# 128 tokens of expert 0 computed during the gating of the last batch

## The chip, the cores and the metric

One core of one Trainium2 chip. The time is the device time of one execution in microseconds; the span is the time from the first to the last instruction of the profiled execution. Inputs are drawn once, so the number of tokens of each expert is fixed.

## What is computed

Causal attention with a decay bias over 4 batches of 8 heads and 576 tokens, then a mixture of 8 experts with one expert for each token, then a dense feed-forward layer with a squared ReLU. The weights of the last layer come as float64.

```python
# attention: scores + min(-(cum_i - cum_j), 0), causal, softmax, times v
x = attn_out.transpose(0, 2, 1, 3).reshape(2304, 512)
logits = x @ w_gate
e_idx = argmax(logits, axis=1)                 # one of 8 experts
gate_w = softmax(logits)[e_idx]; eom = sigmoid(x @ w_output_gate)
for e in range(8):
    h = maximum(x[e_idx == e] @ w1[e], 0)      # 512 -> 1024
    out[e_idx == e] = gate_w * eom * (h @ w2[e])   # 1024 -> 512
g = maximum(out @ w_in, 0) ** 2                # 512 -> 2048
result = g @ w_out                             # 2048 -> 512
```

With these inputs expert 0 gets 334 tokens: 252 from the first three batches and 82 from the last.

## The kernel before

**Order.** The order of the instructions is written out by hand: `at(key, fn)` puts a step on a list, the list is sorted by key, and each engine runs its instructions in that order. Steps on other engines are kept apart by semaphores. In the attention part a key counts work units of head pairs (16 pairs, 7 units each). In the expert part a key counts h blocks: expert g has the steps 8g to 8g + 7.

**Attention and gating.** As soon as a batch of attention is done, `emit_gate` finds for each token its expert and its rank among the tokens of that expert (`s_lg` to `s_rk`), marks ranks in one-hot tiles (`s_r1`, L789) and turns them into a table of token numbers by small matmuls (`s_tb`, L799). The table has three chunks of 128 ranks for each expert. For batches 0 to 2 all this lies beside the attention of the next batch. For the last batch nothing lies beside it: `s_tbl` adds the earlier batches' table, and `gather(0, [c])` fetches the rows of expert 0 for chunk c from DRAM by an indirect DMA on POOL (L289). In the waits TensorE runs dummy products of 512 columns (`warm` L348, `warm_h` L1462).

**Ranking of the experts.** Expert 0 is always first. The other seven are sorted by their number of tokens (`perm_steps`), since each place in the order has a fixed capacity: `CAPS`, 352, 320, 304, 304, 288, 288, 272 and 256 columns. The result is the tile `slot_v`: which expert has which place and where its output starts. SyncE reads it into registers (`load_regs`, L182), seven for the experts and later seven for the places, ahead of the weight loads that use them. `p_tbl` sorts the table itself (`tbl_p`) for the gathers of the later experts.

**Experts.** `x_trans` transposes the gathered rows (L1116) and splits them into a high and a low float32r half on ScalarE (L1122) and the vector engine (L1127). `emit_h` (L1211) makes 128 of the 1024 hidden units by 12 matmuls: 3 products of halves times 4 pieces of 128 inputs. The weights are the stationary operand, the tokens are the moving columns. `emit_hv` (L1221, L1222) applies the ReLU and splits again, and `emit_y` (L1253), two steps behind, adds 12 matmuls into four accumulators. These are called blocks of 12 below. `y_store` puts the result transposed into `yT_d`, sorted by place.

**Weights.** Those of expert g + 1 are loaded during expert g, eight jobs of 512 KB on SyncE's queue (L232), through three staging buffers and one spare. Each job is split into halves by ScalarE (L241) and the vector engine (L245). Beside them 16 pieces of the float64 weights of the last layer are converted (`cv_load` to `cv_store`, every 3.55 steps from step 1.2). The gather of expert 1 (`gather(1)`) uses the only tile for gathered rows.

**PSUM.** In attention the eight banks belong to three rings (`s`, `s2`, `t`). In the expert part they are `z0` to `z7`: four accumulators and a ring of four.

Of the kernel before, what the change touches and what calls it, by code (L numbers as in the profile page):

```python
# [24 lines left out]
P = 128  # L25
# [46 lines left out]
    cvb=0.4,  # L72
    cvm=0.7,
    cvp=3.55,
    cv0=1.2,
# [12 lines left out]
def attention_moe_ffn_kernel(  # L88
# [72 lines left out]
    gap = const.tile([P, 1], F32, name="gap")  # L161
    slot_v = const.tile([1, 3, E], I32, name="slot_v")
# [117 lines left out]

    def gather(g, cs=None):
        if cs is None or cs[0] == 0:
            xr_t[g] = xr_p.tile([P, CH, DM], F32, tag="xr", name="xr")
        t = xr_t[g]
        for c, n in enumerate(rows_of(g)):
            if cs is not None and c not in cs:
                continue
            idx = tbl_i[0:n, c * E:c * E + 1] if g == 0 else tbl_p[0:n, c, g:g + 1]
            nc.gpsimd.indirect_dma_start(  # L289
                out=t[0:n, c, :], out_offset=None, in_=x_d[:, :],  # L290
                in_offset=bass.IndirectOffsetOnAxis(ap=idx, axis=0))
# [10 lines left out]

    with tc.manual_schedule():
        with ExitStack() as actx:
# [7 lines left out]
            ps_s = actx.enter_context(tc.tile_pool(name="ps_s", bufs=K_["S"], space=PSUM))  # L312
            ps_t = actx.enter_context(tc.tile_pool(name="ps_t", bufs=6 - K_["S"] - K_["O"], space=PSUM))
            ps_o = actx.enter_context(tc.tile_pool(name="ps_o", bufs=K_["O"], space=PSUM)) if K_["O"] else ps_t
# [411 lines left out]
            def emit_gate(b, tg, gk):  # L726
# [36 lines left out]
                def s_pr():  # L763
                    pr = ps_o.tile([P, 512], F32, tag=o_tag, name=o_tag)
# [4 lines left out]
                    for t in range(NB - 1):  # L769
                        nc.tensor.matmul(  # L770
                            prv[:, t + 1:NB], lhsT=onesb, rhs=oh[:, t:t + 1].to_broadcast([P, NB - 1 - t, E]),
                            start=False, stop=(t == NB - 2))

# [12 lines left out]
                def s_r1(t, c0=0, c1=CH):  # L786
                    if t == 0 and c0 == 0:
# [4 lines left out]
                def s_tb(c0=0, c1=CH):  # L792
                    tb = T["tb", c0] = bank("o")
# [64 lines left out]
                steps = [s_lg, s_mx, s_eq, s_cand, s_ix, s_oh, s_pr, s_oid, s_tm, s_rk]  # L858
                if last:
# [7 lines left out]
                else:  # L867
                    steps += [partial(s_r1, t) for t in range(NB)] + [s_tb, s_tbl]
                rest = [s_cs, s_ca, s_dl, s_zs, s_pe, s_se, s_rr, s_gq]
                if last:  # L870
                    late_steps.extend(rest[2:])
                    steps += rest[0:2]
                else:
                    steps += rest
                for i, st_ in enumerate(steps):
                    at(tg + (0.001 * i if last else gk[i]), st_)
                if last:
                    at(tg + 0.0055, warm, K_["wm"][3])
                    at(tg + 0.0145, warm, K_["wm"][4])
# [193 lines left out]
            for i, job in enumerate((k, i, h) for k, i in half_jobs(0, "a") + half_jobs(0, "b") for h in range(2)):  # L1073
# [3 lines left out]
                at(tw + 0.5, part_lo, *job)  # L1077
            emit_tasks()

        stg_p = ctx.enter_context(tc.tile_pool(name="stg", bufs=3))  # L1080
# [6 lines left out]
        ps_z = ctx.enter_context(tc.tile_pool(name="ps_z", bufs=1, space=PSUM))  # L1087
        ring = [4, 4, 0]

        def bank_z(i):  # L1090
            return ps_z.tile([P, 512], F32, tag=f"z{i}", name=f"z{i}")

        def bank_x():
            ring[2] += 1
            return bank_z(ring[0] + ring[2] % ring[1])

# [11 lines left out]
        xp_t = {}  # L1108

        def x_pe(g, c, k0=0, k1=KD):  # L1110
            if c == 0:
                xt_t[g] = xt_p.tile([P, 2, KD, TT], F32R, tag="xt", name="xt")
            r = rows_of(g)[c]
            ps = bank_x()
            for kk in range(k0, k1):
                nc.tensor.transpose(  # L1116
                    ps[:, (kk - k0) * r:(kk - k0 + 1) * r], xr_t[g][0:r, c, kk * P:(kk + 1) * P], ident[0:r, 0:r])
            xp_t[g, c, k0] = ps[:, 0:(k1 - k0) * r].rearrange("p (k n) -> p k n", k=k1 - k0)

        def x_hi(g, c, k0=0, k1=KD):  # L1120
            r = rows_of(g)[c]
            nc.scalar.copy(out=xt_t[g][:, 0, k0:k1, c * P:c * P + r], in_=xp_t[g, c, k0])  # L1122

        def x_lo(g, c, k0=0, k1=KD):
            r = rows_of(g)[c]
            xt = xt_t[g]
            nc.vector.tensor_tensor(  # L1127
                out=xt[:, 1, k0:k1, c * P:c * P + r], in0=xp_t.pop((g, c, k0)),
                in1=xt[:, 0, k0:k1, c * P:c * P + r].bitcast(F32), op=ALU.subtract)
# [73 lines left out]
        def emit_h(g, e, f, fl):  # L1203
            n = sum(rows_of(g))
# [12 lines left out]
        def emit_hv(g, f):  # L1217
            n = sum(rows_of(g))
# [21 lines left out]
        def emit_y(g, e, f, fl, nf, f0=0):  # L1240
# [5 lines left out]
            if g < E:  # L1246
                n = CAPS[g]
# [47 lines left out]
        def emit_yv(g):  # L1295
            ysb = ysb_t[g] = y_p.tile([P, 4, TT], F32, tag="ysb", name="ysb", bufs=1)
            if g < E:
                n = CAPS[g]
# [13 lines left out]
        def y_store(g):  # L1312
            ysb = ysb_t.pop(g)
            if g < E:
                n = CAPS[g]
                dst = yT_d.rearrange("(k p) n -> p k n", p=P)
                nc.sync.dma_start(
                    out=dst[:, :, 0:n] if g == 0 else dst[:, :, ds(reg_o[g], n)], in_=ysb[:, :, 0:n])
# [9 lines left out]

        scr = {}

        def gt2(nm, shape, rows=P):
            if not scr:
                scr["t"] = y_p.tile([P, 4, TT], F32, tag="ysb", name="ysb", bufs=1).rearrange("p a n -> p (a n)")
                scr["n"] = 0
            n0 = scr["n"]
            scr["n"] = n1 = n0 + int(np.prod(shape))
# [350 lines left out]
```

## Time and profile before

| | |
|---|---|
| median of 3 runs | 877.02 us (875.78 to 878.04) |
| profiled execution | 876.1 us |
| its span | 874.3 us |
| TensorE matmul busy | 846.9 us, 97% |
| vector engine busy | 521.5 us, 60% |
| ScalarE busy | 449.7 us, 51% |
| GpSimd (POOL) busy | 254.5 us, 29% |
| DMA moved | 113.13 MB |
| mean granted TensorE clock | 0.991 |

Times in the rows below are microseconds from the start of the span unless they are marked ns. PE is TensorE, PEld its weight loads, DVE the vector engine, ACT ScalarE, SP SyncE. A busy time is that of an engine as a whole; a matmul's record overlaps the next one, so the cost of a stream of matmuls is read from starts, or from the chain of work. L12 is line 12 of the kernel.

### The profile page before, as it was taken

Reading aid. Unit: us, or ns where it says so; the run is one execution under the profiler, and the core shown is the slowest. Engines: PE = TensorE matmul, PEld = TensorE weight load, DVE = VectorE, ACT = ScalarE, POOL = GpSimd, SP = SyncE. Lnnn points to the kernel's source line nnn. Section 1 sums busy time; section 2 is a strip of 40 time slices with the busy share of each in tenths; the row PEclk is TensorE's granted clock in tenths of the full one; section 3 lists DMA queues with packets and bytes.
Section 4 is the critical chain, followed back from the end, with each engine's and each line's share of the span. In section 5 each row is a group of like instructions: output and inputs, shape, how many; then the busy total and the mean of one; then the engine's idle time right before and its main releaser. Section 6 shows DMA issues by size and latency. Waiting matters only on the chain.

```text
span 874.3 us, 15070 instructions
## 1 busy us (share of the span) xinstructions
PE 846.9 (97%) x5381; PEld 750.2 (86%) x5381; DVE 521.5 (60%) x1182; ACT 449.7 (51%) x1001; POOL 254.5 (29%) x302
## 2 busy tenths in 40 slices
PE   7999999999899999999999999999999999999993
PEld 5877777776589999999999999999999999999993
DVE  8667777978666687777866667664333333232221
ACT  6687878987254566565655546443333232222221
POOL 4322344543125655556302232331101001001001
PEclk9999999999999999999999999999999999999997
DMA  6666677652178798988983433321010110000001
GB/s 157 142 161 140 150 178 177 171 135 79 47 243 273 237 265 235 281 267 254 293 231 118 145 108 109 97 85 61 25 49 36 47 63 37 1 1 37 0 1 39
DMA packets 112500, 113.13 MB, mean 129 GB/s; under 512 B 66017, under 2 KB 83425, under 8 KB 112418
## 3 DMA queue, kind: packets, MB, share of 16 engines
q1 hardware_dynamic: 106162, 97.23, 40.4%
q0 software_dynamic: 3664, 9.62, 3.2%
q10 hardware_dynamic: 2592, 5.24, 1.7%
q8 instruction: 44, 0.72, 0.4%
q14 instruction: 38, 0.31, 0.1%
HBM read 80.50 MB, written 23.32 MB: 119 GB/s over the span
## 4 chain that ended last, share of the span: by engine, by line
PE 55%; issue 30%; ACT 5%; DVE 4%; POOL 3%; DMA 1%; SPq 1%; POOLq 0%; DVEq 0%; ACTq 0%
PE z L1211 19%; PE z L1253 12%; PE z L1262 7%; PE t L580 5%; PE s L483 4%; PE t L543 4%; ACT p L527 2%; POOL out_dram L1321 2%; ACT sta L423 1%; PE z L1116 1%; PE t L396 1%; ACT pt L562 1%; PE s L618 1%; PE t L675 1%; DMA stg<-in_moe_w_dram 1%
## 5 line engine op out<-in xcount | busy, mean ns | idle before, releaser
L1211 PE MATMUL z<-xt,w 128*128 128x384 f32 (+6 forms) x1920 | 334.2, 323 | 0.4 <-DVE h L1222 0.4
L1211 PEld LDWEIGHTS z<-xt,w 128*128 128x128 f32 x1920 | 312.3, 188 | 9.3 <-DVE h L1222 0.6
L1262 PE MATMUL z<-w,h 128*128 128x512 f32 x864 | 214.9, 393 | 0.0
L1262 PEld LDWEIGHTS z<-w,h 128*128 128x128 f32 x864 | 160.7, 188 | 29.3
L1231 DVE SCALAR_TENSOR_TENSOR r<-z,r 128x384 f32<-128x384 f32 x96 | 53.3, 556 | 128.4 <-ACT r L1230 127.5
L1230 ACT ACTIVATE r<-z 128x384 f32<-128x384 f32 x96 | 47.1, 491 | 149.9 <-PE z L1211 147.6
L1253 PE MATMUL z<-h,w 128*128 128x304 f32 (+5 forms) x768 | 115.0, 299 | 0.0
L1253 PEld LDWEIGHTS z<-h,w 128*128 128x128 f32 x768 | 108.0, 188 | 0.0
L1179 POOL TENSOR_TENSOR cvm<-cvm,cva 128x512 f32<-128x512 f32 x32 | 43.6, 1363 | 195.3 <-DVE cva L1175 153.8
L1238 DVE TENSOR_TENSOR h<-r,h 128x384 fp32r<-128x384 f32 x96 | 60.9, 635 | 50.3 <-ACT h L1237 47.4
L1321 POOL DMA_INDIRECT out_dram<-ysb,tok_m x18 | 17.4, 968 | 245.5 <-ACT ysb L1308 183.2
L527 ACT ACTIVATE p<-p,nm 128x128 f32<-128x128 f32 (+3 forms) x144 | 84.2, 589 | 4.8 <-DVE nm L510 4.7
L1237 ACT CAST h<-r 128x384 fp32r<-128x384 f32 x96 | 49.3, 513 | 63.3 <-DVE r L1231 63.0
L510 DVE CUSTOM_DVE_ANT_0 p<-s,mask 128x128 f32<-128x128 f32 (+3 forms) x128 | 59.6, 486 | 28.8 <-PE s L483 27.7
L543 PE MATMUL t<-ident,p 128*128 128x128 f32 x400 | 69.4, 283 | 3.1 <-DVE sta L427 1.1
L245 DVE TENSOR_TENSOR w<-stg,w 128x1024 fp32r<-128x1024 f32 x49 | 68.7, 1401 | 0.8 <-ACT w L241 0.8
L543 PEld LDWEIGHTS t<-ident,p 128*128 128x128 f32 x400 | 44.5, 141 | 19.7 <-ACT p L527 7.3
L241 ACT CAST w<-stg 128x1024 fp32r<-128x1024 f32 x49 | 51.3, 1046 | 8.7 <-DMA stg<-in_moe_w_dram 6.0
L1222 DVE SCALAR_TENSOR_TENSOR h<-z,h 128x304 fp32r<-128x304 f32 (+5 forms) x64 | 29.6, 462 | 42.0 <-ACT h L1221 41.3
L444 POOL CAST stb<-sta 64x1152 fp32r<-64x1152 f32 x28 | 31.4, 1149 | 79.5 <-PE s L483 47.4
L1180 POOL TENSOR_TENSOR cvm<-cvs,cvm 128x512 f32<-128x512 f32 x32 | 53.3, 1666 | 2.5
L483 PE MATMUL s<-sta 128*64 128x288 f32 (+4 forms) x204 | 49.8, 341 | 3.4 <-ACT sta L423 1.3
(219 smaller groups left out, 1025.7 us busy)
## 6 DMA issues: line engine op xcount, KB each, us to landing
stg<-in_moe_w_dram SPq DMA_DIRECT2D x42, 512.0 KB
cv<-in_moe_w_out_dram SPq DMA_DIRECT2D x16, 512.0 KB
stx<-in_moe_w_dram SPq DMA_DIRECT2D x14, 512.0 KB
cv<-in_moe_w_in_dram SPq DMA_DIRECT2D x14, 512.0 KB
xr<-yT_d SPq DMA_DIRECT2D x8, 768.0 KB
qk<-in_q_dram SPq DMA_DIRECT2D x32, 128.0 KB
qk<-in_k_dram SPq DMA_DIRECT2D x32, 128.0 KB
v<-in_v_dram SPq DMA_DIRECT2D x32, 128.0 KB
```

The lines of the kernel that those rows point to most:

```text
L241: nc.scalar.copy(out=w_parts(job)[0], in_=raw[job])
L245: nc.vector.tensor_tensor(out=lo, in0=raw.pop(job), in1=hi.bitcast(F32), op=ALU.subtract)
L483: nc.tensor.matmul(ps[0:mw, d0:d0 + nn], lhsT=ql[r, m0:m0 + mw], rhs=kl[r, c0:c0 + nn], start=(i == 0 and (tail or n == 0)), stop=(done an ...
L510: nc.vector.tensor_tensor_reduce(out=dst, in0=src, in1=msk, scale=-1.0, scalar=3.0e38, op0=ALU.add, op1=ALU.min, accum_out=nm[:, c:c + 1])
L527: nc.scalar.activation(out=pt[:, cs], in_=pt[:, cs], func=AF.Exp, scale=-1.0, bias=nm[:, c:c + 1], accum_out=rs[:, r:r + 1])
L543: nc.tensor.transpose(tp[:, i * P:(i + 1) * P], pt[:, j0:j0 + P], ident)
L1180: nc.gpsimd.tensor_tensor(out=m, in0=sq, in1=m, op=ALU.add)
L1211: nc.tensor.matmul(ps[:, 0:n], lhsT=wa[:, zw, kk, fl * P:(fl + 1) * P], rhs=xt[:, zx, kk, 0:n], start=(i == 0), stop=(i == 3 * KD - 1))
L1231: nc.vector.scalar_tensor_tensor(out=gg, in0=ps[:, 0:TT], scalar=0.0, in1=gg, op0=ALU.max, op1=ALU.mult)
L1238: nc.vector.tensor_tensor(out=ht[:, 1], in0=gg, in1=ht[:, 0].bitcast(F32), op=ALU.subtract)
L1253: nc.tensor.matmul(y_acc[g][d][:, 0:n], lhsT=wb[:, zw, fl, d * P:(d + 1) * P], rhs=ht[:, zh, 0:n], start=(f == 0 and i == 0), stop=(f == n ...
L1262: nc.tensor.matmul(acc, lhsT=ht[:, zh, c * P:(c + 1) * P], rhs=wb[:, zw, fl, :], start=(first and i == 0), stop=(last and i == 2))
```

## The change

The first three batches already fix the 128 first ranks of expert 0. Their row numbers are copied to `idx0` after the gating of batch 2 and gathered in the last head pair (from the part of `x_d` that the first three batches wrote). In the gating of the last batch these 128 tokens go through both layers of expert 0, with the tokens as the stationary operand and 512 weight columns moving: `early_h` (two halves of 12 matmuls), `early_hr`, `early_ht`, `early_hs` (ReLU, transposes, split), `early_y` (24 matmuls into one bank), `early_copy` and `early_store`. Tiles of finished head pairs hold the operands. The eight `z` banks are opened ahead of this gating instead of behind attention. The dummy products `wm[3]` to `wm[8]` go.

Expert 0 itself then has 224 columns (`cols_of`) instead of 352, from chunks 1 and 2. The order within the gating is new: ranks, table and gather of chunk 1, then chunk 2, then the counts and the ranking of the experts (`p_cnt`, `p_first`), then chunk 0 of the table, which only later experts need, and `p_tbl`. The rest of the ranking's small operations (`m_ov`, `m_off`, `m_cnt`, `m_end`) are spread over the steps 2.95 to 5.95, and `pos_tokens` goes from step 1.5 to 6.95. One more condition (`seen0`) sends the kernel to its general loop if the first three batches have fewer than 128 tokens of expert 0. The registers are read one per expert, each ahead of the loads of that expert. The conversion of the last layer's weights starts at step 4.0 with 3.45 steps between pieces, and the transposes of expert 1's rows come 1.2 steps later.

```diff
-    cvp=3.55,
-    cv0=1.2,
+    cvp=3.45,
+    cv0=4.0,
...
+    def cols_of(g):
+        return sum(rows_of(g)) - P * first_of(g)
...
-            idx = tbl_i[0:n, c * E:c * E + 1] if g == 0 else tbl_p[0:n, c, g:g + 1]
+            if g == 0:
+                idx = tbl_i[0:n, c * E:c * E + 1] if c else idx0
+            else:
+                idx = tbl_p[0:n, c, g:g + 1]
...
                 if last:
-                    ahead = 2
-                    for c in range(CH):
-                        steps += [partial(s_r1, t, c, c + 1) for t in range(ahead if c else 0, NB)]
-                        steps.append(partial(s_tb, c, c + 1))
-                        if c + 1 < CH:
-                            steps += [partial(s_r1, t, c + 1, c + 2) for t in range(ahead)]
-                        steps += [partial(s_tbl, c, c + 1), partial(gather, 0, [c])]
...
+                    eh, ey = partial(early_h, 0), partial(early_h, 1)
+                    steps += [partial(eh, 0, 9), *pr, s_n3, partial(eh, 9, 12), partial(early_hr, 0), partial(ey, 0, 5)]
+                    steps += [*r1[1], tb[1], partial(early_ht, 0), *r1[2][0:2], tl[1], partial(gather, 0, [1])]
+                    steps += [partial(early_hs, 0, 0), partial(ey, 5, 8), *r1[2][2:], tb[2], partial(ey, 8, 12)]
+                    steps += [partial(early_hr, 1), s_cs, s_ca, p_cnt, tl[2], partial(gather, 0, [2]), s_dl]
+                    steps += [partial(early_hs, 0, 1), partial(early_y, 0, 2), partial(early_ht, 1)]
+                    steps += [partial(early_hs, 1, 0), partial(x_pe, 0, 1), start_scr, *p_first, partial(early_y, 2, 4)]
+                    steps += [partial(early_hs, 1, 1), *r1[0], partial(x_pe, 0, 2)]
+                    steps += [partial(early_y, 4, 8, ((0, 0), (0, 1))), tb[0], partial(early_y, 4, 8, ((1, 0),))]
+                    late_steps.extend([tl[0], p_tbl, *rest[3:]])
...
+                if b == B - 2:
+                    at(tg + gk[16] + 0.05, nc.vector.tensor_copy, idx0, tbl[:, 0:1])
+                    at(tg + gk[16] + 0.06, gather, 0, [0])
...
-                    at(tg + 0.0055, warm, K_["wm"][3])
-                    at(tg + 0.0145, warm, K_["wm"][4])
...
+            def early_h(half, i0, i1):
+                if i0 == 0:
+                    EA["h", half] = bank_z(3 + half)
+                wa = half_views((0, "a"))
+                seq = [(zw, zx, kk) for zw, zx in ((0, 0), (1, 0), (0, 1)) for kk in range(KD)]
+                for i in range(i0, i1):
+                    zw, zx, kk = seq[i]
+                    nc.tensor.matmul(
+                        EA["h", half], lhsT=x0[:, zx, kk], rhs=wa[:, zw, kk, 512 * half:512 * half + 512],
+                        start=(i == 0), stop=(i == 3 * KD - 1))
...
+            te = len(K_["order"]) * (NPAIR - 1)
+            at(te + K_["ext"], early_xt)
+            at(te + K_["exs"], early_xs)
...
+            emit_tasks(NU * (NPAIR - 1) + K_["lpv"][0][-1] + K_["xe"] + 0.01 - 1e-6)
+            pctx.close()
+            zp.append(ctx.enter_context(tc.tile_pool(name="ps_z", bufs=1, space=PSUM)))
...
-        at(-0.74, load_regs, range(1, E), 0, reg_e, E - 1)
-        for i, fn in enumerate(late_steps + then):
+        at(-1.1, load_regs, [1], 0, reg_e, E - 1)
+        for i, fn in enumerate(late_steps[0:2]):
+            at(-0.7 + 0.01 * i, fn)
+        for i, fn in enumerate(late_steps[2:]):
             at(-0.5 + 0.01 * i, fn)
...
-        at(0.3, gather, 1)
+        for i, fn in enumerate(p_late):
+            at(2.95 + i, fn)
+        for c in (1, 2):
+            at(-1.0 + 0.1 * c, x_hi, 0, c)
+            at(-0.99 + 0.1 * c, x_lo, 0, c)
+        at(-0.65, early_copy)
+        at(0.5, early_store)
+        at(-0.6, gather, 1)
...
+            if g:
+                at(n0 + NF + 1.0, load_regs, [g], 1, reg_o, NT)
+            if g > 1:
+                at(n0 - NF - 1.5, load_regs, [g], 0, reg_e, E - 1)
...
-                w_job(job, max(ta - K_["wld"], -0.7), ta + K_['wh'], ta + K_['wl'])
-        at(1.5, pos_tokens)
+                w_job(job, -0.7 if g == 0 and i < 4 else ta - K_["wld"], ta + K_['wh'], ta + K_['wl'])
+        at(6.95, pos_tokens)
```

## Rows read from the trace of the kernel before

**Rows 1.** The page, busy tenths in 40 slices of the span:
```profile
PE   7999999999899999999999999999999999999993
...
DMA  6666677652178798988983433321010110000001
```
**Rows 2.** TensorE in order of time: start us, us, engine, line, operation:
```profile
220.53 1.90 PE L580 MATMUL t<-pt,v 128*64 128x320 f32 x20
...
223.82 2.32 PE L348 MATMUL t<-onesb 128*128 128x512 bf16 x10
225.98 0.18 PE L766 MATMUL t<-carryb,onesb 128*128 128x40 bf16 x1
...
227.68 0.63 PE L799 MATMUL t<-oid_all,r 128*128 128x8 bf16 x14
...
230.45 2.32 PE L1462 MATMUL z<-onesb 128*128 128x512 bf16 x5 [0.26 <-DVE tbl_i L808]
...
237.76 6.15 PE L1211 MATMUL z<-xt,w 128*128 128x352 f32 x36
```
**Rows 3.** Busy time by stretch: length, PE, PEld, DVE, ACT, POOL, granted clock, DMA:
```profile
224.00:228.00 4.00, 4.00 (x35) 2.07 (x33) 3.35 (x19) 1.89 (x10) 0.32 (x1) 1.00 0.27 78
228.00:230.00 2.00, 1.56 (x23) 0.98 (x20) 1.85 (x11) 0.00 (x0) 1.22 (x1) 1.00 0.00 0
230.00:234.00 4.00, 3.74 (x15) 2.00 (x16) 0.62 (x4) 0.22 (x1) 2.35 (x4) 0.57 0.60 176
...
252.00:272.00 20.00, 19.88 (x125) 19.59 (x126) 16.70 (x23) 11.42 (x18) 8.05 (x6) 1.00 0.76 254
```
**Rows 4.** Chain of work: start us, us, what (352, 272, 256, 512 columns):
```profile
262.62 1.93 PE z L1253 x12
...
340.17 0.44 PE z L1116 x4
...
424.07 1.50 PE z L1211 x12
...
447.59 1.44 PE z L1211 x12
...
465.35 2.08 PE z L1262 x9
```
**Rows 5.** TensorE in expert 0 and at expert 1's first block, in order of time:
```profile
246.07 0.63 PE L1116 MATMUL z<-ident,xr 128*128 128x128 f32 x4 [0.23 <-DMA xr<-x_d,tbl_p]
...
251.08 0.66 PE L1116 MATMUL z<-ident,xr 128*128 128x128 f32 x4 [0.54 <-DMA xr<-x_d,tbl_p]
252.12 2.19 PE L1211 MATMUL z<-xt,w 128*128 128x352 f32 x12 [0.39 <-DVE h L1222]
...
268.25 1.93 PE L1211 MATMUL z<-xt,w 128*128 128x320 f32 x12
```
**Rows 6.** The vector engine in order of time:
```profile
219.25 0.69 DVE L564 COPY pt<-t 128x512 f32<-128x512 f32 x1
220.64 0.42 DVE L564 COPY pt<-t 128x256 f32<-128x256 f32 x1 [0.69 <-PE t L543]
...
239.19 0.16 DVE L1390 CAST slot_v<-ysb 1x8 int32<-1x8 f32 x1
...
251.98 1.22 DVE L245 TENSOR_TENSOR w<-stg,w 128x1024 fp32r<-128x1024 f32 x1
...
262.63 1.93 DVE L245 TENSOR_TENSOR w<-stx,w 128x1024 fp32r<-128x1024 f32 x1
```
**Rows 7.** ScalarE in order of time, end of attention and gating:
```profile
221.34 0.48 ACT L562 COPY pt<-t 128x384 f32<-128x384 f32 x1 [2.06 <-PE t L580]
...
223.74 2.15 ACT L661 ACTIVATE xs<-s,rca 128x64 f32<-128x64 f32 x10 [0.89 <-DVE lw L637]
```
**Rows 8.** POOL, then SyncE's queue, in order of time:
```profile
228.71 1.22 POOL L289 DMA_INDIRECT xr<-x_d,tbl_i  x1 [2.32 <-DVE r L789]
...
244.48 5.00 SPq L232 DMA_DIRECT2D stg<-in_moe_w_dram  x3
```

More of the change, by code (lines that the diff above doesn't have):

```diff
@@ L72 @@
     cvb=0.4,
+    ext=4.4,
+    exs=5.6,
     cvm=0.7,
-    cvp=3.55,
-    cv0=1.2,
+    cvp=3.45,
+    cv0=4.0,
     cvl=2.5,
@@ new lines, in attention_moe_ffn_kernel, with p_cnt, gt2 @@
+    R = {}
+    def p_cnt():
+        cps = bank_x()
+        nc.tensor.matmul(cps[:, 0:E], lhsT=onesb, rhs=carryb, start=True, stop=True)
+        R["cps"] = cps[:, 0:E]
+    scr = {}
+    keep = {"pv": "eq", "sv": "cand", "pm": "lg"}
+    def gt2(nm, shape, rows=P):
+        if nm in keep:
+            v = g_p.tile([P, 80 if keep[nm] == "lg" else 40], F32, tag=keep[nm], name=keep[nm])
+            n0, n1 = 0, int(np.prod(shape))
+            return split(v[0:rows, n0:n1], shape)
+        if "t" not in scr:
+            scr["t"] = y_p.tile([P, 4, TT], F32, tag="ysb", name="ysb", bufs=1).rearrange("p a n -> p (a n)")
+            scr["n"] = 0
+        n0 = scr["n"]
+        scr["n"] = n1 = n0 + int(np.prod(shape))
+        return split(scr["t"][0:rows, n0:n1], shape)
@@ L772, in s_pr, with s_n3 @@
                             start=False, stop=(t == NB - 2))
+                def s_n3():
+                    nc.scalar.copy(out=seen0, in_=T["pr"][0:1, 0, 0:1])
                 def s_oid():
@@ L786, in s_r1 @@
                 def s_r1(t, c0=0, c1=CH):
-                    if t == 0 and c0 == 0:
+                    if "r1" not in T:
                         T["r1"] = r1_p.tile([P, NB, CH * P], BF16, tag="r1", name="r1")
@@ new lines, in early_hr, with early_ht, early_hs @@
+            def early_hr(half):
+                EA["r", half] = qk_p.tile([P, 2 * QM + 2 * D], F32, tag="qk", name="qk")[:, 0:512]
+                nc.scalar.activation(out=EA["r", half], in_=EA["h", half], func=AF.Relu)
+            def early_ht(half):
+                ps = EA["t", half] = bank_z(half)
+                for i in range(4):
+                    nc.tensor.transpose(ps[:, i * P:(i + 1) * P], EA["r", half][:, i * P:(i + 1) * P], ident)
+            def early_hs(half, z):
+                ps = EA["t", half].rearrange("p (k n) -> p k n", k=4)
+                f = slice(4 * half, 4 * half + 4)
+                if z == 0:
+                    nc.scalar.copy(out=hT0[:, 0, f], in_=ps)
+                else:
+                    nc.vector.tensor_tensor(
+                        out=hT0[:, 1, f], in0=ps, in1=hT0[:, 0, f].bitcast(F32), op=ALU.subtract)
@@ new lines, in early_y @@
+            def early_y(f0, f1, zs=((0, 0), (0, 1), (1, 0))):
+                if "y" not in xp_t:
+                    xp_t["y"] = bank_z(2)
+                wb = half_views((0, "b"))
+                for zh, zw in zs:
+                    for f in range(f0, f1):
+                        nc.tensor.matmul(
+                            xp_t["y"], lhsT=hT0[:, zh, f], rhs=wb[:, zw, f, :],
+                            start=(f == 0 and zh == zw == 0), stop=(f == FE // P - 1 and zh == 1))
+            te = len(K_["order"]) * (NPAIR - 1)
```

293 lines of the change are left out of this document (155 added, 138 removed).

## Prediction

> **What bounds the kernel now.** I read the slices of the page first. TensorE is busy in nine tenths or more of nearly every slice, and the DMA engines are at seven to nine tenths from slice 12 to 21, where the experts run [rows 1]. So the time is TensorE's own work plus the few places where that work isn't useful. Next I read TensorE in order of time around the gating of the last batch [rows 2]. The last product of attention ends at 222.4 us (220.53 + 1.90), the transposes behind it end at 224.0, and the first block of expert 0 starts at 237.76. In these 13.8 us TensorE runs 29 dummy products of 512 columns (L348 and L1462), the small products of the ranking, and 12 transposes. The chain here goes through the vector engine and a gather, not through TensorE. Busy time by stretch shows the same [rows 3]: from 228 to 230 us TensorE is busy 1.56 of 2.00 us with small table products, and from 230 to 234 us its granted clock is 0.57, near the lower of its two levels (1.2 GHz); before and after it is 1.00, the upper one (2.4 GHz).
>
> From 237.76 us the chain is one block of 12 matmuls after another with almost no gap. A block costs 1.93 us at 352 columns, 1.50 at 272 and 1.44 at 256; nine products of 512 columns cost 2.08; four 128 x 128 transposes cost 0.44 [rows 4]. Expert 0 is 16 such blocks: eight h and six y blocks lie before expert 1's first block at 268.25, two y blocks behind it. Its cost is 268.25 - 237.76 + 2 x 1.93 = 34.35 us [rows 2, 4, 5].
>
> **The change, part by part.** The 128 earliest tokens of expert 0 come from the first three batches, so their rows are known before the last batch is gated. Their two layers move into the 13.8 us.
>
> *Removed.* The 29 dummy products. They held nothing up for more than about 2.3 us [rows 2], but they fill the gap, and real work takes their place.
>
> *Added to the gap.* 24 products of 512 columns for h and 24 for y: 48 x 0.231 = 11.1 us (0.231 is 2.08/9 [rows 4]). Eight transposes of h and eight of the two late chunks of x at 0.11: 1.75. The ranking and table products stay: 30 at 0.63/14 = 0.045 are 1.35 [rows 2], and the counts add some 0.2. Sum 14.4 us. Against this stands the other chain. The table of chunk 1 is first now; in before its counterpart went to the gather at 228.71, and transposed rows were at hand some 4 us later [rows 8]. In the new order, writing the engines' queues out with durations from the rows, chunk 1 is gathered at about 229 and wanted at 233.5, chunk 2 is gathered at 230.5 and wanted at 235. TensorE becomes the bound of this stretch and doesn't wait: the new end is its start plus 14.4.
>
> *The start moves too.* The early x must be transposed and split in the last head pair: one transposed group in a gap of TensorE, one copy on ScalarE, one 0.69 us subtraction on the vector engine. The latter is queued ahead of the two copies at 219.25 and 220.64 [rows 6]. The first copy then ends about 1.35 us later, the second about 0.65 (it had 0.69 us of idle ahead of it). The product at 220.53 runs over that second copy; after its own first 0.7 us it needs it, so I charge 0.5 us, between nothing and 0.7. The ScalarE copy lies in that engine's idle 2.06 us [rows 7] and costs nothing. Start 224.5, expert 0 at 238.9: **1.1 us later** than now.
>
> *Expert 0 shrinks* from 352 to 224 columns. No row has 224. From 352 to 272 a column costs (160.8 - 125.0)/80 = 0.45 ns per matmul, from 272 to 256 only (125.0 - 120.0)/16 = 0.31, and a transpose with 128 columns against a full 128 x 128 weight tile still costs 110 [rows 4]. So the curve flattens: a straight line gives 106 ns, the cost of 256 columns gives 120. I take 114, since the last slope is already lower than the line's. 192 x 0.114 = 21.9 us. Add 12 transposes of expert 1 (1.3), four of the early result on its way out (0.44), and 1.0 of stalls; the stalls now are 0.23, 0.54 and 0.39 [rows 5], from the gather of expert 1 and from ScalarE waiting for weights. Sum 24.6 against 34.35: **9.7 us less**.
>
> The Trainium skill, "TensorE: Matmul & The Clock Gate", section "LDWEIGHTS (loading the stationary operand)", gives a weight load a time that depends only on its columns, 128/1.2 = 107 ns. By it an estimate of 192 x 0.107 = 20.5 us would be the least that expert 0 can cost, and a further cut of columns would bring nothing; the bend between 272 and 256 agrees with it, while no row here shows the floor itself.
>
> *Registers, ranking, weights.* The ranking of the experts now runs on the vector engine before the last table, so the slots are known near 233.7 instead of 239.3 [rows 6]. One register is read instead of seven ahead of the first weights, which were issued at 244.48 [rows 8]; now about 234.5, except that the third staging buffer lies on memory which the early h occupies until 238.9, and SyncE's queue holds the fourth behind it. Expert 1's weights thus have more lead than before, and expert 0 being 10 us shorter doesn't starve it. The other registers are read one per expert on SyncE, each in front of that expert's loads; a read there is under a microsecond and the queue is ahead of need. The gather of expert 1 is held until the early result has left its tile (about 240.8), yet was issued at 242.45 before; its transposes are 1.2 steps later as well.
>
> *Vector engine.* Twenty small operations (0.16 each, as the cast at 239.19 [rows 6], 3.2 us) move from the quiet start of expert 0 into its steps 3 to 7. From 252 to 272 us the vector engine is busy 16.70 of 20.00 [rows 3], weight splits taking 1.22 to 1.93 each [rows 6]. The same work, 0.8 less for narrower h, plus 3.2, is 19.1 us in a stretch that TensorE now does in 15. The overhang is 4 us. An h block's low half is wanted some 4.7 blocks after it, 6.4 us, so I cost the overhang at nothing beyond the 1.0 of stalls.
>
> **Sum.** 9.7 - 1.1 = 8.6 us less. The profiled execution took 876.1 us (span 874.3), so 867.5; the median of the runs is 0.9 above it, so **868.4 us**.
>
> **Rivals.**
> *The weight-load floor:* 224 columns cost what 256 do, 0.120. For it: the bend. Against: the transposes' 0.110. 192 x 0.006 = 1.1 more: 869.5. The skill page above is the rule behind it.
> *The vector engine becomes the bound in expert 0:* the 4 us of overhang come through in place of the 1.0 charged: 871.4. For it: 16.70 of 20.00. Against: the 6.4 us of slack.
> *Banks not free:* the early products want accumulators that ScalarE's ten scaled copies (223.74 + 2.15) still read [rows 7]. The stream starts 1.9 us later: 870.3. Against: those copies read another ring than the first early h.
> *The clock:* on the other side. If TensorE is granted the lower level over the early stream, as it was from 230 to 234 us [rows 3], 14.4 us of work double: 868.4 + 14.4 = 882.8, slower. It decides once more than 8.6 us, 60% of the stream, run at that level; half the stream gives 875.6, no change. Against: the fall followed small table products, and the stream is now dense.
>
> **How the numbers follow.** Forecast 0.57, floor 0.12, vector engine 0.17, banks 0.06, clock over half 0.04, over all 0.04. Low end: pitch 106 (-1.5), early products at a dummy's (225.98 - 223.82)/10 = 0.216 [rows 2] (-0.7), no late start (-0.5), no stalls (-1.0): 864.7, so 864.5. High end: the floor (+1.1) with the vector overhang (+3.0) and a little: 873.0. This leaves out the clock cases and some of the tails. A measurement of this kernel can tell about 0.3% (2.6 us) from no change: faster 0.92, same 0.04, slower 0.04.
>
> **What would show it.** TensorE without an idle stretch from 224 to 239 us at granted clock 1.00; expert 0's blocks at 1.37 us; expert 1's first h block near 260; everything behind it the same length, shifted by about 8.6 us. It is wrong if blocks stay at 1.44 or more, if expert 0's blocks wait on the vector engine or on DMA, if TensorE waits for the gathered chunks, or if a later expert, whose weights share DMA engines already at nine tenths, gives some of it back.

## The result: slower, and the profile after

The changed kernel takes 888.02 us (median of 4 runs, 881.3 to 890.66), the kernel before in the same comparison 877.06 (875.78 to 878.04). The ratio is 1.0113, 95% interval 1.0085 to 1.0141: 1.1% slower, where 1.0% faster was forecast. The profiled execution took 888.55 us (span 886.9).

I cut both spans at the same seven events and subtracted. The last column is the kernel of the eighth experiment ("all mends"), put here so that the stages need be listed only once.

| stage, us | before | after | after - before | all mends |
|---|---|---|---|---|
| up to the last head pair's first product (x20) | 209.64 | 210.75 | +1.11 | 212.02 |
| to the end of attention's last transposes | 14.34 | 15.32 | +0.98 | 14.74 |
| gate: to expert 0's first block | 13.78 | 17.74 | +3.96 | 14.06 |
| expert 0, to expert 1's first block | 30.49 | 26.29 | -4.20 | 22.06 |
| expert 1 | 29.94 | 32.28 | +2.34 | 28.79 |
| experts 2 and 3 | 56.05 | 56.05 | 0.00 | 56.06 |
| experts 4 and 5 | 53.57 | 61.44 | +7.87 | 53.59 |
| experts 6 and 7 | 49.70 | 49.81 | +0.11 | 49.82 |
| dense layers | 416.8 | 417.2 | +0.4 | 417.3 |
| span | 874.3 | 886.9 | +12.6 | 868.4 |

The first row isn't the change's: this stage took between 209.4 and 212.0 us in the traces of all kernels here, and longest in that of the fastest.

The slices of the page of after, to be read against [rows 1]:

```profile
PE   7999999999889999998999999999999999999993
...
DMA  6676677652178887988894442331020120000001
```

TensorE now has eights in the slices of 222 to 266 us (gate, expert 0) and of 399 to 421 us (expert 5). Before it had one eight here, in the slice of 219 to 240 us, and nines behind it.

TensorE of after in order of time: start us, us, engine, line, operation, and in brackets the idle time ahead of it and what ended it. These answer to [rows 2, 5].

```profile
222.25 0.44 PE L691 MATMUL t<-ident,p 128*128 128x128 f32 x2 [0.69 <-DVE pt L712]
222.62 1.90 PE L728 MATMUL t<-pt,v 128*64 128x320 f32 x20
...
228.04 3.34 PE L1064 MATMUL z<-w,sta 128*128 128x512 f32 x9 [1.97 <-ACT xs L809]
...
243.81 1.50 PE L1419 MATMUL z<-xt,w 128*128 128x224 f32 x12
...
254.32 0.63 PE L332 MATMUL z<-ident,xr 128*128 128x128 f32 x4 [1.88 <-DMA xr<-x_d,tbl_p]
...
267.32 1.60 PE L1419 MATMUL z<-xt,w 128*128 128x224 f32 x12 [1.40 <-DVE xt L1335]
...
290.18 3.29 PE L1419 MATMUL z<-xt,w 128*128 128x320 f32 x12 [1.91 <-DVE h L1430]
...
377.76 2.02 PE L1419 MATMUL z<-xt,w 128*128 128x288 f32 x12 [1.96 <-DVE h L1430]
...
405.08 2.02 PE L1419 MATMUL z<-xt,w 128*128 128x288 f32 x12 [2.51 <-DVE h L1430]
```

Four things are to be seen. The new subtraction stands ahead of a copy and costs TensorE 0.69 us at 222.25. The early stream doesn't begin behind attention's transposes at 226.07 but 1.97 us later, released by the last of ScalarE's scaled copies, `xs`. Expert 0 has two stops of over a microsecond (1.88 and 1.40) and three of 0.35 to 0.50, 4.6 us in all. And TensorE stops for 1.9 to 2.5 us once in expert 1 and twice in experts 4 and 5, where little of the change lies but the new timing of the conversion of the last layer's weights.

Busy time by stretch in the gate of after: length, PE, PEld, DVE, ACT, POOL, granted clock, DMA share, GB/s (compare [rows 3]):

```profile
226.00:228.00 2.00, 0.07 (x1) 0.00 (x0) 1.69 (x10) 1.99 (x10) 0.00 (x0) 1.00 0.14 42
228.00:230.00 2.00, 1.96 (x7) 1.59 (x8) 0.08 (x1) 0.00 (x0) 0.32 (x1) 0.77 0.41 109
230.00:232.00 2.00, 2.00 (x12) 1.28 (x10) 0.31 (x2) 0.11 (x1) 0.00 (x0) 0.50 0.03 4
232.00:234.00 2.00, 2.00 (x14) 1.47 (x13) 1.31 (x8) 0.64 (x2) 0.00 (x0) 0.88 0.00 0
```

Behind the idle stretch TensorE's granted clock goes to 0.50, the lower of its two levels, while it is busy all the time. The first nine early products take 3.34 us; where the clock stays at 1.00 the same record shows 2.31 (third experiment).

The clock falls again behind each of the three later stops. The stretches of the lowest clock there:

```profile
292.00:294.00 2.00, 2.00 (x9) 2.00 (x8) 2.00 (x4) 0.53 (x3) 1.81 (x3) 0.52 0.36 51
...
380.00:382.00 2.00, 2.00 (x11) 2.00 (x10) 2.00 (x4) 1.76 (x3) 1.84 (x2) 0.50 0.78 230
...
408.00:410.00 2.00, 2.00 (x10) 1.72 (x9) 2.00 (x4) 0.00 (x0) 1.89 (x2) 0.50 0.81 281
```

With the neighbouring stretches (granted clocks 0.63 and 0.52; 0.82, 0.50 and 0.83; 0.64 and 0.50), what TensorE loses is 2.0 us times the sum of what is missing from 1.00: 1.7 us each time. So the 7.87 us of experts 4 and 5 are stops of 1.96 and 2.51 us and 3.4 us of low clock. In expert 1 it is a stop of 1.91 and 1.7 of low clock.

The chain of waits of after, from expert 0 on: start us, us, what. Between the lines the chain is TensorE's blocks and short steps of ScalarE, the vector engine and POOL.

```profile
246.40 9.87 DMA yT_d<-h
...
256.35 0.36 ACT h L1429
...
279.01 9.09 DMA w_in_d<-cvm
...
368.71 7.04 DMA w_out_d<-cvm
...
395.41 8.14 DMA w_out_d<-cvm
```

Before, the chain here was one block after another. Now it runs through four DMA stores of 256 KB. The first is the early result on its way out: it holds one of the three `h` tiles until 256.27, and ScalarE, whose next ReLU wants that tile, stands for 7.40 us:

```profile
256.35 0.36 ACT L1429 ACTIVATE h<-z 128x224 fp32r<-128x224 f32 x1 [7.40 <-PE z L1419]
```

The record names the product that feeds the ReLU, but that had been done since 248.4 us; the chain gives the store, and the fourth experiment bears it out. The other three are converted pieces of the last layer's weights. There is one `cvm` tile; ScalarE's multiplication for the next piece must wait until the store of the last has read it, and ScalarE's queue keeps its order, so the ReLUs behind it wait too, then the vector engine, then TensorE.

What SyncE's queue of after waited for between 232 and 262 us (us in total, times, longest us), then the queue itself in order of time, to be read against 244.48 of [rows 8]:

```profile
SPq L186 <- DVE slot_v L402: 11.1, 1, 11.1
SPq L236 <- PE z L1092: 3.1, 1, 3.1
```
```profile
244.12 1.46 SPq L236 DMA_DIRECT2D stg<-in_moe_w_dram  x3
```

All of expert 1's first weights are issued at 244.12, when the last early product (L1092) is done, not near 234.5. So 2 MB of weights, the gather, the early store and the first pieces to be converted move together: from 244 to 254 us the DMA share is 0.90.

### The profile page after: what moved, and what is told of

It is laid out like the page before. It is cut to its first block, busy times and chain, and to the rows that moved or that the text cites. A ratio compares the mean times of both kernels' runs of the same rounds, so it can differ in the third digit from the quotient of the medians.

```text
span 886.9 us, 15158 instructions
## 1 busy us (share of the span) xinstructions
PE 848.3 (96%) x5412; PEld 752.7 (85%) x5412; DVE 525.1 (59%) x1186; ACT 452.4 (51%) x1008; POOL 260.8 (29%) x302
## 4 chain that ended last, share of the span: by engine, by line
PE 51%; issue 29%; ACT 6%; DVE 5%; DMA 4%; POOL 3%; POOLq 0%; ACTq 0%; DVEq 0%; SPq 0%
PE z L1419 17%; PE z L1461 9%; PE z L1470 7%; PE t L728 5%; PE s L631 4%; PE t L691 4%; ACT p L675 2%; POOL out_dram L1529 2%; DMA w_out_d<-cvm 2%; DMA yT_d<-h 1%; ACT sta L571 1%; DMA w_in_d<-cvm 1%; PE t L544 1%; PE z L1064 1%; ACT pt L710 1%
## 5 line engine op out<-in xcount | busy, mean ns | idle before, releaser
L249 DVE TENSOR_TENSOR w<-stg,w 128x1024 fp32r<-128x1024 f32 x49 | 71.7, 1466 | 3.9 <-ACT w L245 3.9
L1388 POOL TENSOR_TENSOR cvm<-cvs,cvm 128x512 f32<-128x512 f32 x32 | 55.8, 1744 | 2.5
```

The costliest lines, as they stand in the source:

```text
L249: nc.vector.tensor_tensor(out=lo, in0=raw.pop(job), in1=hi.bitcast(F32), op=ALU.subtract)
L1388: nc.gpsimd.tensor_tensor(out=m, in0=sq, in1=m, op=ALU.add)
```

## The experiments

**Theory:** five separate costs were missed. (a) Opening the new PSUM banks waits for every reader of the old ones. (b) The stop makes the clock fall. (c) The staging buffers wait in the same way for the early operands, so that expert 1's loads collide with everything else of expert 0. (d) The early result's store holds an `h` tile. (e) Converting pieces from step 4.0 every 3.45 steps makes ScalarE wait for stores. **Rivals:** the conversion alone; the vector engine in expert 0; or the early computation itself costs more than it saves, in which case no mend of its surroundings makes it faster than before. Each kernel is an edit of the changed one unless it says otherwise. Line numbers are those of the changed kernel.

### The conversion as it was

```diff
-    cvp=3.45,
-    cv0=4.0,
+    cvp=3.55,
+    cv0=1.2,
```

> The changed kernel with the old timing of the float64 conversion (first piece at step 1.2, one every 3.55 steps). Theory C: in the changed kernel ScalarE waits in its order for the store of the piece before (25.1 us of idle ahead of L1375, against 13.6 us in the kernel before), since 3.45 steps leave 1.15 instead of 1.25 steps between a store and the next use of its only tile; the ReLU behind it is late, TensorE stops, and 7.9 us are lost in experts 4 and 5. Then the old timing gives 879 to 882 us and no stop of TensorE in experts 4 and 5. Rival D: the shorter expert 0 loads the DMA engines more and any timing stalls; then it stays at 886 to 890 us.

876.66 us (874.54 to 882.69), ratio 1.0010 (0.9992 to 1.0028), faster than the theory expected. Experts 4 and 5 take 53.59 us and expert 1 28.79. So all of the 7.87 us, and more than the 2.34, hang on these two numbers. Expert 0 is no shorter than in after (26.42 against 26.29). It stops for another reason now; ScalarE and TensorE of this kernel in order of time:

```profile
250.66 0.68 ACT L1371 ACTIVATE cvs<-cv 128x512 f32<-128x512 f32 x1 [5.97 <-DMA cv<-in_moe_w_in_dram]
```
```profile
251.63 1.15 PE L1461 MATMUL z<-h,w 128*128 128x224 f32 x8 [3.05 <-ACT h L1429]
```

The earlier conversion waits for its own load, which moves in the same crowd as the weights.

### The change's conversion in the kernel before

```diff
-    cvp=3.55,
-    cv0=1.2,
+    cvp=3.45,
+    cv0=4.0,
```

> The kernel before with nothing changed but the timing of the conversion (first piece at step 4.0, one every 3.45 steps). Theory C: the stops in the later experts appear here too, without any early tokens: 882 to 887 us. Rival D: 877 us, no difference.

877.91 us (876.41 to 882.59), ratio 1.0023 (1.0008 to 1.0039), between the rival's 877 and the theory's 882 and nearer to the rival. TensorE of this kernel:

```profile
396.04 1.85 PE L1211 MATMUL z<-xt,w 128*128 128x288 f32 x12 [2.34 <-DVE h L1222]
```

One stop of 2.34 us, and experts 4 and 5 take 56.33: the interval costs the kernel before 2.8 us there, and 1.1 come back in expert 0 (29.35 in place of 30.49). So the conversion does harm by itself, but a third of what it does in the changed kernel. The traces show what the third is: one stop in place of two, and the granted clock stays at 1.00 behind it. Why the changed kernel gets more stops from the same interval isn't shown.

### Banks that wait tile by tile

```diff
-            zp.append(ctx.enter_context(tc.tile_pool(name="ps_z", bufs=1, space=PSUM)))
+            zp.append(ctx.enter_context(tc.tile_pool(name="ps_z", bufs=1, space=PSUM, reuse_waits="tile")))
```

> The changed kernel with the eight z banks waiting bank by bank for their last use in attention, not for the last use of any bank of the pools they replace. Theory P: the 1.97 us wait of the first early product for ScalarE's scaled copies is such a wait of the whole pool, the bank itself was free; then the early stream starts 2.0 us sooner, TensorE isn't idle ahead of it, its clock stays at 1.00 and another 1.9 us come back: 884 us if the later experts pass it on. Rival: the bank is really in use, and the wait stays.

881.24 us (879.97 to 883.15), ratio 1.0048 (1.0032 to 1.0065). TensorE of this kernel:

```profile
226.03 2.31 PE L1064 MATMUL z<-w,sta 128*128 128x512 f32 x9
```

The stop is gone, nine products take 2.31 us, and the granted clock is 1.00 throughout 226 to 240 us. The gate, counted here and below from the last x20 product to expert 0, takes 17.55 us in place of 21.19. The bank of the first early product belonged to the ring `s2`, which the copies `xs` don't read; only the way in which a new pool takes over memory tied it to `xs`. In the traces, which differ by 5.4 us (the medians by 6.8), most of the rest is in experts 4 and 5, which take 58.92 in place of 61.44.

### The early store from another tile

```diff
-            t = h_p.tile([P, 2, TT], F32R, tag="h", name="h").rearrange("p a n -> p (a n)")[:, 0:KD * P].bitcast(F32)
+            t = scr["t"][:, 1024:1024 + KD * P]
```

> The changed kernel with the early result leaving from a part of the scratch tile instead of one of the three h tiles. Theory H: the 9.87 us transfer of the early result holds one of the three h tiles, so ScalarE's third ReLU of expert 0 starts 7.4 us late; with its own place the wait goes, and expert 0 gets 2 to 4 us shorter: 884 to 886 us. Rival: the DMA engines set the pace of expert 0 and the wait moves to the gathered rows (now 1.88 us) or to weights that land late: under 1 us, 887 to 888 us.

880.57 us (875.9 to 885.78), ratio 1.0044 (1.0022 to 1.0067). ScalarE's 7.40 us before the third ReLU are gone, but expert 0 gains only 1.82 us (24.47). TensorE still stops for the gathered rows, 1.88 us at 254.32 in after and here:

```profile
253.84 0.63 PE L332 MATMUL z<-ident,xr 128*128 128x128 f32 x4 [2.04 <-DMA xr<-x_d,tbl_p]
```

Behind this stop the granted clock falls to 0.50 (256 to 258 us), which it doesn't in expert 0 of after; this takes back 1.7 us of the gain. The store was one of several transfers that came late together; with it out of the way the gather is left.

### Staging buffers that wait tile by tile

```diff
-        stg_p = ctx.enter_context(tc.tile_pool(name="stg", bufs=3))
+        stg_p = ctx.enter_context(tc.tile_pool(name="stg", bufs=3, reuse_waits="tile"))
...
-            hT0 = early_view(st_a[(NPAIR - 3) % 3], [2, FE // P, P])
+            hT0 = early_view(st_b[(NPAIR - 2) % 2], [2, FE // P, P])
```

> The changed kernel with the staging buffers waiting tile by tile for the memory that they take over, and the early h in a tile that no staging buffer covers. Theory P (a new pool waits for the last use of the whole old one): the first weights of expert 1, issued at 244.12 behind the last early product, are issued about 240, as soon as the register is read; the transfers of expert 0 (four weight loads, the early result, a conversion load, the gather) then collide less, and expert 0 takes 24 to 25 us to the first block of expert 1 where it took 26.3. Rival: the staging buffers were free, and SyncE's queue waits for something else: still behind the last early product. The time stays between 881 and 889 us, since the conversion's timing is not touched.

879.62 us (875.47 to 884.49), ratio 1.0044 (1.0023 to 1.0065). SyncE's queue of this kernel:

```profile
238.22 1.48 SPq L236 DMA_DIRECT2D stg<-in_moe_w_dram  x3
```

The loads start 5.9 us sooner than in after, about 3 us ahead of expert 0 (241.49) rather than with it. Expert 0 takes 22.40 us and its stops are 0.83 and 0.50, although the early store still uses an `h` tile. So (c) is the cause of most of expert 0's stops, and (d) costs little once the loads are early. Experts 4 and 5 still take 60.59.

### The subtraction behind the copies

```diff
-    exs=5.6,
+    exs=6.7,
```

> The changed kernel with the split of the early x moved behind the two copies of probabilities that it now goes ahead of (from 5.6 to 6.7 units of the last head pair). Theory X: the 1.0 us by which the end of attention moves (from the products of the pair before to the last transposes 14.34 us in the kernel before, 15.32 in the changed one) is this subtraction; it then takes 14.3 to 14.5. Rival: the transposes of the early x or the new gather cost it; then it stays at 15.3. The whole time 884 to 889 us.

884.6 us (882.02 to 885.69), ratio 1.0090 (1.0069 to 1.0112). The vector engine of this kernel:

```profile
222.77 0.69 DVE L1055 TENSOR_TENSOR sta<-s,sta 128x512 fp32r<-128x512 f32 x1 [1.27 <-ACT sta L1054]
```

It now lies in idle time of its engine. TensorE no longer stops ahead of the last products, and the end of attention takes 14.73 us in place of 15.32: 0.6 of the 0.98. The edit moves ScalarE's copy of the early x too, which now stands ahead of its copies `oT`; TensorE waits 0.26 us for those behind its last products, part of the 0.4 that is left. The gate is as in after, stop and low clock included.

### A slower conversion

```diff
-    cvp=3.45,
+    cvp=3.75,
```

> The changed kernel with one conversion piece every 3.75 steps instead of 3.45, the first still at step 4.0. Theory C: 1.45 steps between a store and the next use of its tile are more than in the kernel before, so TensorE doesn't stop in experts 1, 4 and 5 (now 32.3 us and 61.4 us, then 29 to 30 and 53.6): 876 to 879 us. Rival: it is the start of the conversion, or which transfers it meets, and not the distance: 882 us or more.

876.23 us (873.86 to 878.7), ratio 0.9998 (0.9985 to 1.0011). Expert 1 takes 28.77 and experts 4 and 5 53.59, the start at 4.0 being the change's own: with this start the interval decides whether TensorE stops. (A start at 1.2 with the interval 3.45 wasn't run.) ScalarE's multiplication by kernel, the changed one first: line, operation, count, busy us, mean ns, idle us ahead of it and what ended it.

```profile
L1375 ACT ACTIVATE cvm<-cv 128x512 f32<-128x512 uint16 x32 | 21.6, 675 | 25.1 <-DMA w_in_d<-cvm 13.2 <-DMA w_out_d<-cvm 11.9
```
```profile
L1375 ACT ACTIVATE cvm<-cv 128x512 f32<-128x512 uint16 x32 | 21.6, 675 | 13.4 <-DMA w_in_d<-cvm 8.4 <-DMA w_out_d<-cvm 4.8
```

ScalarE's waits for stores halve. They don't go to zero, and that costs TensorE nothing. Even the longest of them is followed by no stop:

```profile
288.42 0.68 ACT L1375 ACTIVATE cvm<-cv 128x512 f32<-128x512 uint16 x1 [4.20 <-DMA w_in_d<-cvm]
```

So the length of one wait doesn't decide alone; how far ahead the finished `h` blocks are when it comes must matter too, which no run tells apart.

### All mends

The edits of the third to seventh experiment together: banks, store tile, staging, late subtraction, interval 3.75.

> The changed kernel with five edits together: banks, place of the early result, staging, late split, and one conversion piece every 3.75 steps. If the costs found singly are separate and add up, against the changed kernel: 2.0 for the banks, up to 1.9 for the clock, 1.0 for the split, 2 to 3 in expert 0, 10 in experts 1 to 5, so 870 to 872 us. Rival D: DMA sets the pace of experts 0 and 1, and what is won ahead of them is waited for there: 875 us or more, no better than the kernel before.

868.03 us (867.5 to 870.15), ratio 0.9902 (0.9885 to 0.9918): faster than both kernels. TensorE of this kernel:

```profile
226.59 2.31 PE L1064 MATMUL z<-w,sta 128*128 128x512 f32 x9
...
240.82 1.50 PE L1419 MATMUL z<-xt,w 128*128 128x224 f32 x12
242.16 0.60 PE L1577 MATMUL z<-ident,xr 128*128 128x128 f32 x4
242.51 2.92 PE L1419 MATMUL z<-xt,w 128*128 128x224 f32 x24
...
249.94 0.63 PE L332 MATMUL z<-ident,xr 128*128 128x128 f32 x4 [0.49 <-DMA xr<-x_d,tbl_p]
...
260.11 1.60 PE L1419 MATMUL z<-xt,w 128*128 128x224 f32 x12 [0.49 <-DVE xt L1335]
```

From 226.59 to 240.82 the early stream runs without a stop, and expert 0 has none above 0.5 us. This rules out the rival that the early computation costs more than it saves. The mends alone gave 6.8, 7.4, 8.4, 3.4 and 11.8 us, 37.8 in sum; together they give 20.0. They must share what they take away. In the traces of the first four, experts 4 and 5 are also shorter than in after (by 2.5, 3.9, 0.9 and 1.2 us), and the interval alone puts these right. But the changed kernel's own runs lie between 881.3 and 890.66 us, and two traces of one kernel differ there by 4.9 us (two experiments on), so how much of these four figures is the mends' and how much the execution's isn't shown.

### The slower conversion in the kernel before

```diff
-    cvp=3.55,
-    cv0=1.2,
+    cvp=3.75,
+    cv0=4.0,
```

> The kernel before, with nothing of the change but a conversion that starts at step 4.0 and takes a piece every 3.75 steps. Theory: the slower conversion only undoes what the change's 3.45 did; the kernel before had no stop of over 2 us from it, so it is worth at most the stops of expert 0 and 1 there, about 1 us: 875.5 to 877. Rival: the slower conversion is itself the gain of the mended kernel, whatever is done in the gating: 868 to 871, with the starts of expert 1 and 2 as they are before.

876.83 us (874.8 to 880.35), ratio 1.0001 (0.9982 to 1.0019). Nothing: the gain of the mended kernel isn't the conversion's.

### All mends, but the change's interval

```diff
-    cvp=3.75,
+    cvp=3.45,
```

against the kernel with all mends.

> All mends, but the change's own conversion, a piece every 3.45 steps. Theory: the interval itself is too short for the DMA engines while experts 4 and 5 run, so ScalarE waits there for a store again, experts 4 and 5 take 56 to 60 us in place of 53.6, and the time is 871 to 876. Rival: the stops came from everything being late behind the gate; with that mended the short interval costs nothing: 53.6 us and 868.

875.9 us, ratio 0.9993 (0.9976 to 1.0009). The execution with a trace was the shortest of ten, 869.36; the other nine took 875.1 to 880.7. In the trace experts 4 and 5 take 55.06 us, with one stop of 1.21. The median agreed with the theory, but the trace, of an execution about as long as with all mends, shows little of it. I ran the same kernel for a second trace.

> All mends with the change's own interval of 3.45 steps once more, for a second trace: nine of ten executions took 875 to 881 us, the one with a trace 869.4. Theory: the extra 6 us are ScalarE waiting for stores of converted pieces, then TensorE for ScalarE: this execution takes 874 to 879 us, experts 4 and 5 take 58 to 61 us in place of 55.1 (or expert 1 over 31), with idle TensorE of 2 us behind the vector engine's h, and everything up to expert 1 is as in the first trace. Rival: the gate or expert 0 varies, with the clock or the gather; then expert 1 starts 3 us or more later than 260.1 and experts 4 and 5 take 55.

874.68 us. Up to expert 1's first block the two traces agree within 0.15 us (260.28 and 260.13). Then expert 1 takes 30.08 in place of 29.56 and experts 4 and 5 59.94 in place of 55.06, which is all of the 5.4 us between the spans. ScalarE of the second trace, then TensorE:

```profile
277.64 0.67 ACT L1375 ACTIVATE cvm<-cv 128x512 f32<-128x512 uint16 x1 [4.56 <-DMA w_in_d<-cvm]
...
364.02 0.66 ACT L1375 ACTIVATE cvm<-cv 128x512 f32<-128x512 uint16 x1 [4.93 <-DMA w_out_d<-cvm]
...
390.02 0.66 ACT L1375 ACTIVATE cvm<-cv 128x512 f32<-128x512 uint16 x1 [3.73 <-DMA w_out_d<-cvm]
```
```profile
279.70 2.02 PE L1419 MATMUL z<-xt,w 128*128 128x320 f32 x12 [1.24 <-DVE h L1430]
...
366.00 1.84 PE L1419 MATMUL z<-xt,w 128*128 128x288 f32 x12 [2.22 <-DVE h L1430]
...
391.52 2.95 PE L1419 MATMUL z<-xt,w 128*128 128x288 f32 x12 [2.25 <-DVE h L1430]
```

Each of these three waits of ScalarE is followed by a stop of TensorE that is 1.5 to 3.3 us shorter (4.56 - 1.24, 4.93 - 2.22, 3.73 - 2.25). That much the finished `h` blocks cover. Behind the last stop the granted clock falls to 0.50 (392 to 394 us), and the twelve products of 391.52 take 2.95 us in place of 1.84; behind the stop of 2.22 it stays at 1.00. The stops of 2.22 and 2.25 and 1.7 us of low clock make up the 6.35 us by which experts 4 and 5 exceed 53.59, but for 0.2. With the interval at 3.75 and all mends no wait in experts 1 to 5 is above 2.42, and TensorE never stops. At 3.45 it depends on how late a store comes, and one execution of these eleven got through with little.

### Dummy products in the stop

```diff
+                if last:
+                    at(tg + 0.01 - 1e-5, warm, 8)
```

> The changed kernel with eight dummy products of 512 columns, 1.85 us, between the last transposes of attention and the first early product, where TensorE stood for 1.97 us. Theory: that stop is followed by the lower clock, so without it the first nine early products take 2.3 us in place of 3.34, and the gate takes 19.5 to 19.7 us in place of 21.2; the time is about 1.6 less than the changed kernel's. Rival: the lower clock comes whatever TensorE does there, the gate stays at 21.2 and the time at 888.

882.96 us (881.36 to 885.04), ratio 1.0065 (1.0045 to 1.0085). TensorE of this kernel:

```profile
225.37 1.89 PE L496 MATMUL t<-onesb 128*128 128x512 bf16 x8
227.50 2.34 PE L1064 MATMUL z<-w,sta 128*128 128x512 f32 x9 [0.25 <-ACT xs L809]
```

The early stream starts no sooner relative to attention, but its clock is 1.00 throughout and the gate takes 19.64 us in place of 21.19. So the clock's part is 1.55 us and belongs to the stop. (The first and fifth experiment, which have the stop but no fall, take 19.63.) Whether the clock falls after the stop varied: with a stop of 1.96 or 1.97 us it fell in after and in the experiments on the early store, the subtraction and the slower conversion, and stayed at 1.00 in those on the old conversion and on staging. The rest of this kernel's gain lies, by the traces, in expert 1 (29.12) and experts 4 and 5 (59.00), less a longer expert 0 (27.84, with 1.7 us of low clock at 264 to 270 us); why they shift with 1.55 us in the gate stays open. That these stops depend on how stores meet loads is as far as the traces go.

## Why the prediction was wrong, step by step

**What failed** is the step from TensorE's work to the time. The sum took it that this work would run without waits: the early stream "doesn't wait", expert 1's weights come with "more lead than before", 1.0 us of stalls covers the rest, and the conversion has no term. The runs showed in its place stops and low clock that cost 3.3 us in the gate, 4.4 in expert 0, and 11.4 in experts 1, 4 and 5.

**Right.** The new work costs what was worked out. 224 columns cost 1.34 us a block, 0.112 us a matmul, against 0.114 forecast. (The Trainium skill, "TensorE: Matmul & The Clock Gate", section "LDWEIGHTS (loading the stationary operand)", would put a floor at 0.107; 0.112 agrees with that and lies just above it.) In the mended kernel the early stream takes 14.2 us against 14.4, expert 0 with its last two blocks 22.06 + 2 x 1.34 = 24.7 against 24.6, and the median is 868.03 against 868.4. In its trace everything behind the first stage is 8.3 us shorter than before, against 8.6 forecast, so it isn't only the total that agrees. The sum describes a kernel without the five obstacles below. It isn't the change as written: with the change's own interval the other mends bring the median to 875.9 only.

**The end of attention** was charged 0.5 us; it cost 0.98, of which 0.6 goes when the subtraction moves behind the copies. Mis-sized, not misplaced.

**Banks not free** was named with the right price, 1.9 (measured 1.97), and given 0.06. The argument against it, that the first early `h` uses another ring, was true and beside the point: a new pool's tile waits for all tiles of the old pools, not for its own bank's last reader.

**The clock** was a rival with over half the stream at the low level. It was not the stream that brought the low level: in the five traces without the stop ahead of it (third, eighth, tenth with both its traces, dummies) the clock stays at 1.00 over the whole stream, so rivals three and four were one mechanism, 2.0 us and then 1.6. I had weighed them as if independent and had the clock fall for most of the stream or not at all. And nothing in the prediction had it fall outside the stream, where three more stops brought it down for 1.7 us each: with the gate, 6.7 us of the miss are low clock.

**Staging.** "About 234.5, except that the third staging buffer lies on memory which the early h occupies" failed twice. The slots were known at 239.3, not 233.7: 5.1 of these 5.6 us are 1.1 that attention was late, 0.5 more than charged at its end, 2.0 of standing and 1.6 of clock. And the exception held for all three buffers and the one behind them, as it did for the banks. "Expert 1's weights thus have more lead than before" became no lead at all, and this is what filled expert 0 with stops: 26.29 in place of 22.06.

**Early result.** Its store was counted as four transposes, 0.44 us. What it holds was not: an `h` tile for 9.87 us, when the loads are late.

**The conversion** is the largest error, and there was no term for it: 3.45 steps in place of 3.55 stands in the diff and in the description of the change, and the sum passes over it. Experts 4 and 5 lost 7.87 us and expert 1 some 3.5, low clock included (32.28 against 28.77 to 28.79 in the three kernels whose conversion causes no stop). The forecast's last sentence, that a later expert might give some of it back, pointed at the place, but at 1.0 us of stalls and chances of 0.04 it had no weight.

**The vector engine** stopped expert 0 of after for 0.35, 0.50 and 1.40 us, as it worked off what had come late. As a bound of its own it didn't come: with all mends expert 0 stops for it 0.49 us, and for the gather another 0.49, together the 1.0 of stalls that was charged.

So a forecast of -8.6 us in the span became +12.6. The 21.2 between them are 1.1 that attention varied, 0.5 at its end, 3.3 in the gate (17.7 against 14.4), 4.4 in expert 0 (26.3 against 24.6 less its last two blocks), 3.5 in expert 1, 7.9 in experts 4 and 5, and 0.5 behind them.

## What to carry to other kernels

When work moves into a gap, ask of each piece of memory that it touches who must be done before it may be touched, and look at how the pools decide that, not only at who last used those bytes. A step that waits in an engine's queue for a DMA store stops everything behind it, so the number to look at is the time from one use of a single buffer to the next, against the store's time under load; here 9% of the interval decided (3.45 against 3.75 steps). And cost every changed constant of a diff, above all one that has nothing to do with its headline.

## What the runs showed of the hardware

Four stores of 256 KB in after took 7.0 to 9.9 us from issue to release, over stretches in which the profile gives a DMA share of 0.97 to 1.10 (the profile's share can come out above 1), though they are issued by ScalarE and the weight loads by SyncE. The Trainium skill, "DMA: Bandwidth & Descriptors", section "Issuing engines are not separate DMA queues", says that transfers started by ScalarE, SyncE or GpSimd run on the same 16 DMA engines and interleave; these times agree with it. (A later store, issued at 433.14 and waited for until 438.4, took 5.3 us at a share of 0.84.)

A stop of TensorE of 1.97 us ahead of the early stream was followed by the lower clock level in four traces and not in two. In the experts it is the same: the clock fell behind the stops of 1.91, 1.96 and 2.51 us of after, and not behind one of 2.22 (second trace of the tenth experiment) or one of 2.34 (second experiment). So the length of a stop doesn't decide by itself here; a fall cost 1.6 to 1.7 us each time. I had looked for the clock only in long stretches of thin work.

A kernel whose margins are used up doesn't have one time: at 3.45 steps the mended kernel took 869.4 to 880.7 us in eleven executions with the same code, while at 3.75 its four runs lie within 867.5 to 870.2.
